# One tile for the keys and queries of a head pair, wider score matmuls, more buffers and a new order in a block-sparse attention and gated convolution kernel

## The chip, the cores and the metric

The kernel runs on one core of a Trainium2 chip. A core has a matrix engine (TensorE, PE in the profile; its weight loads are the row PEld), a vector engine (VectorE, DVE), a scalar engine (ScalarE, ACT), a general engine (GpSimd, POOL) and a queue engine (SyncE, SP). Data move between the main memory and the on-chip memory by DMA; matmuls write to PSUM. The metric is the device time of one execution in microseconds (us). Three runs of the kernel before took 209.91, 210.04 and 211.36 us, so its median is 210.04 us.

## The reference

Attention over 4 batches of 8 heads, 768 tokens and 64 features is followed by a gated convolution network. Only blocks of 32 x 32 tokens that a mask allows count: the block's own neighbours, the first and last row and column of blocks, and three drawn columns per block row.

```python
scores = scale * np.matmul(q, k.transpose(0, 1, 3, 2))      # 4 x 8 x 768 x 768
mask = np.abs(blk_i - blk_j) <= window
mask = mask | (blk_i == 0) | (blk_j == 0) | (blk_i == n_blocks - 1) | (blk_j == n_blocks - 1)
...                                                          # and three drawn blocks per row
scores = np.where(mask, scores, -1000000000.0)
attn = np.exp(scores - np.max(scores, axis=-1, keepdims=True))
attn = attn / (np.sum(attn, axis=-1, keepdims=True) + 1e-09)
x = np.matmul(attn, v)                                       # heads side by side: 4 x 768 x 512
h = np.maximum(x @ w_in, 0.0)                                # 4 x 768 x 1024
conv_out[t] = sum(conv_w[k] * h[t + k - 1] for k in range(3))
out = (h * 1.0 / (1.0 + np.exp(-conv_out))) @ w_out          # 4 x 768 x 512
```

## The kernel before, in words

The kernel computes all scores densely and folds the mask into the score matmul. The 64 features of a head fill 64 rows of the contraction, and 24 more rows (64 to 87) hold the mask: one row per block row, with -8000 in the queries' part and 0 or 1 in the keys' part. That is why the score matmuls have 88 rows.

**Tiles.** Two heads make a pair; there are 16 pairs, four per batch. For a pair the six chunks of 128 keys and the six chunks of 128 queries are held in two tiles: E_t has the even chunks and O_t the odd ones, each of shape [88, 2, 2, 3, 128] (queries or keys, head, chunk, token). Five such slots are used in turn. The first five pairs get there through transposes on PE (`kq_transposes`: k_tr and q_tr, copied out of PSUM by k_cp and q_cp); pairs 5 to 15 get there through DMA transposes on the SP queue (`kq_crossbar`: xb into a staging tile stg, then two copies stg_cp into E_t and O_t). The mask rows of slots 1 and 2 are copied by DVE (m_slot) and those of slots 3 and 4 by DMAs from SP (m_dma); the last batch gets other query rows through small DMAs (m_last).

**Attention.** A unit is eight blocks of 128 x 128 scores, which fill two PSUM banks (tile st). Each half of a unit is one bank of four blocks (operation s, line 744). ACT takes the exponential of the whole unit (exp, line 755), and PE multiplies the eight blocks with the values (av, line 777). There are 144 units. There are only two st tiles, so the scores of a unit wait for the exponential of the unit two before. Blocks are listed per key chunk: for each key chunk the three query chunks of the half sequence that is at work. Neighbouring blocks of a list are merged into one matmul when they share the key chunk and lie side by side in the same tile:

```python
if pieces and pieces[-1][:4] == (P, hh, kc, par) and pieces[-1][4] + pieces[-1][6] == idx:
    pieces[-1] = pieces[-1][:6] + (pieces[-1][6] + 1,)
```

Here par says even or odd tile and idx the place in it. Of the three query chunks two lie in one tile and one in the other, so a matmul is at most 256 columns wide. A list ends where the PSUM bank ends.

**Behind the attention.** For each pair and half sequence DVE takes the reciprocals and normalizes (rcp, norm, lines 694 and 696), the result is transposed into xT by a DMA transpose on SP (x_xb, line 705) or, in a few places, by PE (x_tr, line 715), and then the first matmul of the network runs (f1, line 893), its relu on ACT or DVE (lines 913 and 915), the three-tap convolution and the gate (mul, add, tanh, g1, g2: mostly DVE, tanh on ACT), the second matmul (f2, lines 808 and 823), the copy out of PSUM (ev, lines 326 and 328) and the store.

**The order.** `put_down` writes the program from a string, ORDER. Each entry names an operation by two characters, then its engine by a letter where there is a choice, then the buffer number for each buffer that it takes. Every engine executes its own operations strictly in that order, and so do the DMA queues of SP, ACT and POOL. Semaphore waits between engines follow from which operations touch which tiles. A planner's costs (the functions t_mm, t_act and so on) and due times stand in the code, but the string alone sets the order.

## Time and profile before

| what | value |
|---|---|
| median of three runs | 210.04 us |
| span of the profiled execution, first to last instruction | 207.2 us |
| median of the runs less that span | 2.8 us |
| PE busy | 196.7 us (95%) |
| ACT busy | 189.4 us (91%) |
| DVE busy | 181.5 us (88%) |
| score matmuls (line 744) | 900 |
| granted clock of TensorE | 1.000 |

The profiled execution's own time is told as its span of 207.2 us; what lies around it, before the first and after the last instruction, is put at the 2.8 us by which the median of the runs exceeds it. A busy share counts the time in which at least one instruction of the engine is at work. Matmuls overlap each other, so the time that a matmul costs is read from the distance between the starts of two neighbours and not from its own duration. In the lines below an arrow names what an idle engine waited for.

### The profile page before, as it was taken

How to read it: one execution, taken by the hardware profiler on the slowest of the kernel's cores; microseconds unless marked ns; L12 is line 12 of the kernel's file. 1: busy time of each engine (PE TensorE's matmuls, PEld its weight loads, DVE VectorE, ACT ScalarE, POOL GpSimd, SP SyncE). 2: the span in 40 equal slices, each digit the busy share in tenths (PEclk: the TensorE clock that was granted, in tenths of full speed). 3: DMA queues.
4: the chain of work that ended last, by engine and by line, in shares of the span. 5: the costliest groups of instructions: out<-in, count | busy, mean ns of one | idle time of the engine just before them, and what ended most of it. 6: DMA issues, size and time to landing. Idle time of an engine off the chain costs nothing.

```text
span 207.2 us, 6783 instructions
## 1 busy us (share of the span) xinstructions
PE 196.7 (95%) x2667; PEld 153.7 (74%) x2687; DVE 181.5 (88%) x571; ACT 189.4 (91%) x248; POOL 60.7 (29%) x113
## 2 busy tenths in 40 slices
PE   7799979989999999999999999999999999999993
PEld 7689858867878877777688767777688877795752
DVE  6877759999699998999999998999799959999950
ACT  6899969999999999999999998999899999998841
POOL 8844355446326124500605292700000000000000
PEclk9999999999999999999999999999999999999999
DMA  6999999999998699993597689992511032100415
GB/s 149 170 207 200 173 169 126 141 135 157 158 151 134 98 138 194 181 190 58 77 167 133 88 103 218 170 213 73 175 43 22 19 121 66 29 11 6 156 50 202
DMA packets 54903, 26.26 MB, mean 127 GB/s; under 512 B 40864, under 2 KB 51832, under 8 KB 54872
## 3 DMA queue, kind: packets, MB, share of 16 engines
q0 software_dynamic: 19984, 11.24, 43.5%
q1 hardware_dynamic: 34312, 13.90, 33.8%
q10 hardware_dynamic: 576, 0.69, 1.0%
q8 instruction: 21, 0.34, 0.7%
q14 instruction: 10, 0.08, 0.2%
HBM read 23.08 MB, written 6.29 MB: 142 GB/s over the span
## 4 chain that ended last, share of the span: by engine, by line
PE 56%; ACT 16%; DVE 16%; DMA 5%; issue 4%; SPq 0%; ACTq 0%
PE st L744 16%; PE mix L893 14%; PE mix L823 14%; ACT pt L755 12%; PE av L777 9%; DVE m L947 5%; DMA xT<-xtok 3%; DVE m L957 3%; DMA o2s<-in_q_dram 2%; DVE hE L915 2%; DVE xtok L696 2%; DVE gT L1004 1%; ACT hE L913 1%; DVE m L999 1%; DVE e L328 1%
## 5 line engine op out<-in xcount | busy, mean ns | idle before, releaser
L755 ACT ACTIVATE pt<-st 128x1024 bf16<-128x1024 f32 x144 | 140.2, 1036 | 5.4 <-PE st L744 5.0
L777 PEld LDWEIGHTS <-pt 128*128 128x128 bf16 x1152 | 53.1, 97 | 11.6 <-issue 0.2
L777 PE MATMUL av<-vt,pt 128*128 128x65 bf16 x1152 | 60.6, 193 | 0.3
L893 PE MATMUL mix<-xT,winb 128*128 128x384 bf16 (+2 forms) x288 | 53.8, 308 | 1.1 <-DMA xT<-xtok 0.9
L947 DVE TENSOR_SCALAR m<-hE,cw 128x382 bf16<-128x382 bf16 (+2 forms) x192 | 49.6, 317 | 0.2
L744 PE MATMUL st<-o 88*128 88x128 bf16 (+1 forms) x240 | 44.3, 229 | 1.1 <-ACT pt L755 0.8
L744 PE MATMUL st<-o,e 88*128 88x128 bf16 (+1 forms) x228 | 43.8, 233 | 0.5 <-ACT pt L755 0.4
L744 PE MATMUL st<-e,o 88*128 88x128 bf16 (+1 forms) x224 | 43.0, 234 | 1.2 <-ACT pt L755 1.2
L823 PE MATMUL mix<-woutb,gT 128*128 128x512 bf16 x156 | 43.1, 379 | 0.8
L744 PE MATMUL st<-e 88*128 88x128 bf16 (+1 forms) x208 | 41.5, 239 | 0.6 <-ACT pt L755 0.5
L744 PEld LDWEIGHTS <-o 88*128 88x128 bf16 x464 | 34.4, 97 | 9.4 <-issue 3.0
L744 PEld LDWEIGHTS <-e 88*128 88x128 bf16 x436 | 33.0, 97 | 7.5 <-issue 1.4
L957 DVE TENSOR_TENSOR m<-m 128x764 bf16<-128x764 bf16 (+2 forms) x64 | 33.8, 532 | 0.4
L893 PEld LDWEIGHTS <-winb 128*128 128x128 bf16 x288 | 23.9, 97 | 8.2 <-issue 1.6
L996 ACT ACTIVATE m<-m 128x764 bf16<-128x764 bf16 (+2 forms) x32 | 26.3, 826 | 0.5 <-DVE m L957 0.4
L415 POOL COPY pace<-pt 1x1 bf16<-1x1 bf16 x24 | 8.3, 347 | 47.3 <-ACT pt L755 47.0
L823 PEld LDWEIGHTS <-gT 128*128 128x128 bf16 x184 | 15.4, 97 | 9.0 <-DVE gT L1004 0.5
L915 DVE TENSOR_SCALAR hE<-mix 128x384 bf16<-128x384 f32 x29 | 15.9, 554 | 4.3 <-PE mix L893 4.1
L696 DVE TENSOR_TENSOR xtok<-av,rcp 128x384 bf16<-128x384 f32 (+2 forms) x36 | 18.2, 506 | 0.3
L1004 DVE TENSOR_TENSOR gT<-m,hE 128x764 bf16<-128x764 bf16 (+3 forms) x36 | 18.1, 508 | 0.3
L913 ACT ACTIVATE hE<-mix 128x384 bf16<-128x384 f32 (+2 forms) x35 | 16.9, 503 | 1.6 <-PE mix L893 1.2
L238 POOL DMA_DIRECT2D nat<-in_q_dram x23 | 16.9, 736 | 3.0 <-issue 2.8
(80 smaller groups left out, 156.4 us busy)
## 6 DMA issues: line engine op xcount, KB each, us to landing
out_dram<-o2s SPq DMA_DIRECT2D x22, 256.0 KB
vn<-in_v_dram POOLq DMA_DIRECT2D x16, 192.0 KB, 5.3
nat<-in_k_dram POOLq DMA_DIRECT2D x15, 192.0 KB, 5.1
nat<-in_q_dram POOLq DMA_DIRECT2D x7, 192.0 KB, 4.8
winb<-in_moe_w_in_dram POOLq DMA_DIRECT2D x2, 512.0 KB, 8.1
woutb<-in_moe_w_out_dram POOLq DMA_DIRECT2D x4, 256.0 KB, 5.8
nat<-in_q_dram POOLq DMA_DIRECT2D x8, 96.0 KB, 5.3
xT<-xtok SPq DMA_TRANSPOSE x32
```

The lines of the kernel that those rows point to most:

```text
L696: nm = op("norm", {"DVE": t_dps(128 * C)}, lambda e: nc.vector.tensor_tensor(out=xtok_t[xk.index][:, 0:C].rearrange("p c h d -> p h c d"), ...
L744: nc.tensor.matmul(out=st[:, 128 * x:128 * (x + n_)], lhsT=QK[kc % 2][s][0:88, 1, hh, kc // 2, :], rhs=QK[par][s][0:88, 0, hh, idx:idx + n ...
L755: nc.scalar.activation(out=pt_t[ptb.index], in_=st_t[stb.index], func=AF.Exp, bias=0.0, scale=0.125)
L777: nc.tensor.matmul(out=o[:, off:off + 65], lhsT=pt_t[ptb.index][:, 128 * x:128 * x + 128], rhs=V_t[vslot_b[P].index][:, hh, kc, 0:65], sta ...
L823: nc.tensor.matmul(out=acc(), lhsT=gT_t[gb.index][:, ffc, 128 * t:128 * t + 128], rhs=woutb[:, ffc, :], start=(ffc == 0), stop=(ffc == NFF ...
L893: nc.tensor.matmul(out=mix_t[hb.index][:, w1 * y:w1 * y + w1], lhsT=winb[:, fc, 128 * ffc:128 * ffc + 128], rhs=xT_t[xt_buf[n].index][:, f ...
L913: i = nc.scalar.activation(out=dst, in_=src, func=AF.Relu, bias=0.0, scale=0.5)
L915: i = nc.vector.tensor_scalar(out=dst, in0=src, scalar1=0.5, scalar2=0.0, op0=ALU.mult, op1=ALU.max)
L947: i = nc.vector.tensor_scalar(out=m_t[cb.index][:, x, y, 0:w], in0=hE_t[heb.index][:, f0 + y, t0 + x:t0 + x + w], scalar1=cw[:, x, f0 + y: ...
L957: nc.vector.tensor_tensor(out=m[:, a_, :, 0:w], in0=m[:, a_, :, 0:w], in1=m[:, b_, :, 0:w], op=ALU.add)
L996: th = [op("tanh", {"ACT": t_act(2 * w) + 0.04}, lambda e, cb=cb, w=w: nc.scalar.activation(out=m_t[cb.index][:, 0, :, 0:w], in_=m_t[cb.in ...
L1004: i = nc.vector.tensor_tensor(out=gT_t[gtb.index][:, f0:f0 + 2, t0:t1], in0=m_t[cb.index][:, 0, :, 0:w], in1=hE_t[heb.index][:, f0:f0 + 2, ...
```

## The change

Four things are changed together.

1. E_t and O_t become two strided views of one tile QK_t of shape [88, 2, 2, 6, 128], in which even and odd chunks alternate. The three query chunks of a half sequence then lie side by side. The query chunks are listed in the order 0, 1, 2 or 3, 4, 5, so that up to three neighbours are merged: the pieces of a bank of four blocks become 384 + 128, 256 + 256 or 128 + 384 columns wide, where they were 256 + 128 + 128 in some order.
2. The mask rows of slots 3 and 4 are copied by one DMA each where there were two, and the last batch's query rows by one DMA per pair where there were two.
3. Seven constants grow: stg 2 to 3, nat 4 to 6, vn 3 to 4, pt 6 to 8, xtok and rcp (one constant) 3 to 4, xT 3 to 4, o2s 4 to 5.
4. ORDER is replaced.

The new ORDER, read entry by entry, holds the same operations apart from the six DMAs fewer. These change their engine, in net numbers: three relus, one ev, one k_cp and three q_cp go from ACT to DVE; one cast_k, one v_cp and one x_cp go from DVE to ACT. ACT's operations up to the first exponential are, before: m_q, m_h1, cast_q, k_cp, cast_k, cast_q, k_cp, k_cp, q_cp, q_cp, m_h1; and after: m_q, m_h1, cast_k, cast_q, m_h1, k_cp, cast_k, q_cp, cast_q, k_cp. DVE's operations around the first two normalizations are, before: rcp, k_cp, he_zero, cw, v_cp, k_cp, k_cp, q_cp, q_cp, norm, v_cp, diag, rcp, diag, diag, norm; and after: rcp, diag, norm, v_cp, k_cp, q_cp, rcp, q_cp, norm. The first f1 stands behind the same number of score and value operations in both. POOL's loads keep their order but for a few neighbours that change places, with as many paces (small copies that hold POOL until a load has landed). At the end of SP's list the stores of two earlier output tiles stand behind those of the last batch's tiles 2 and 3, where before none did.

```diff
-    NSLOT, NSTG, NNAT, NVN, NPT, NXK, NXT, NHE, NCV, NGT, NOS = 5, 2, 4, 3, 6, 3, 3, 2, 4, 2, 4
-
-    E_t = many(NSLOT, [88, 2, 2, 3, 128], BF16, "e")
-    O_t = many(NSLOT, [88, 2, 2, 3, 128], BF16, "o")
+    NSLOT, NSTG, NNAT, NVN, NPT, NXK, NXT, NHE, NCV, NGT, NOS = 5, 3, 6, 4, 8, 4, 4, 2, 4, 2, 5
+
+    QK_t = many(NSLOT, [88, 2, 2, 6, 128], BF16, "qk")
+    E_t, O_t = [[t[:, :, :, x:6:2] for t in QK_t] for x in range(2)]
...
-            else:
-                mr.append(op("m_dma", {"SP": 0.75}, lambda e, t=t, s=s: nc.sync.dma_start(out=t[s][64:88], in_=t[0][64:88]),
-                             T(4.5 * s - 2.5) + 0.1 * x, [m_h1[x], m_kh[x]], dma=("hw", 0.6)))
+        if s >= SLOT_DMA:
+            mr = 2 * [op("m_dma", {"SP": 0.75}, lambda e, s=s: nc.sync.dma_start(out=QK_t[s][64:88], in_=QK_t[0][64:88]),
+                         T(4.5 * s - 2.5), m_h1 + m_kh + m_k, dma=("hw", 0.6))]
...
-                    dcopy(e, t[slot.index][0:64, 1, hs[0]:hs[-1] + 1].rearrange("p h c s -> p (h c s)"), src)
+                    dcopy(e, t[slot.index][0:64, 1, hs[0]:hs[-1] + 1], src.rearrange("p (h c s) -> p h c s", h=len(hs), c=3))
...
-    blk_order = {0: [(0, 0, 0), (0, 1, 2), (1, 0, 1)], 1: [(1, 1, 0), (1, 2, 2), (0, 2, 1)]}
+    blk_order = {0: [(0, 0, 0), (1, 0, 1), (0, 1, 2)], 1: [(1, 1, 0), (0, 2, 1), (1, 2, 2)]}
...
-                if pieces and pieces[-1][:4] == (P, hh, kc, par) and pieces[-1][4] + pieces[-1][6] == idx:
-                    pieces[-1] = pieces[-1][:6] + (pieces[-1][6] + 1,)
+                at = 2 * idx + par
+                if pieces and pieces[-1][:3] == (P, hh, kc) and pieces[-1][3] + pieces[-1][5] == at:
+                    pieces[-1] = pieces[-1][:5] + (pieces[-1][5] + 1,)
...
-                                     lhsT=QK[kc % 2][s][0:88, 1, hh, kc // 2, :],
-                                     rhs=QK[par][s][0:88, 0, hh, idx:idx + n_, :].rearrange("p c s -> p (c s)"),
+                                     lhsT=QK_t[s][0:88, 1, hh, kc, :],
+                                     rhs=QK_t[s][0:88, 0, hh, at:at + n_, :].rearrange("p c s -> p (c s)"),
```

105 lines of the change are left out of this document (51 added, 54 removed).

## The prediction

> **What bounds the kernel now.** I read the busy shares and the chain first, and then the busy time of each engine by stretches of the span, because a share over the whole span hides where an engine has room.
>
> ```profile
> PE 196.7 (95%) x2667; PEld 153.7 (74%) x2687; DVE 181.5 (88%) x571; ACT 189.4 (91%) x248; POOL 60.7 (29%) x113
> PE 56%; ACT 16%; DVE 16%; DMA 5%; issue 4%; SPq 0%; ACTq 0%
> core 0: us, PE busy (x) PEld busy (x) DVE busy (x) ACT busy (x) POOL busy (x), PEclk, DMA share, GB/s
> 7.00:28.00 21.00, 18.41 (x323) 16.70 (x321) 16.61 (x49) 20.82 (x25) 10.51 (x20) 1.00 1.32 190
> 28.00:45.00 17.00, 15.46 (x217) 12.20 (x216) 14.24 (x46) 15.39 (x22) 8.57 (x19) 1.00 1.22 132
> 45.00:190.00 145.00, 143.55 (x1955) 110.83 (x1971) 135.70 (x408) 139.93 (x175) 35.52 (x62) 1.00 0.72 116
> 190.00:204.00 14.00, 13.42 (x125) 8.61 (x124) 9.85 (x42) 8.65 (x20) 0.00 (x0) 1.00 0.34 125
> 204.00:207.20 3.20, 0.00 (x0) 0.00 (x0) 0.00 (x0) 0.12 (x1) 0.00 (x0) 1.00 0.33 113
> ```
>
> The rows tell of three regimes. From 7 to 28 us ACT is busy 20.82 of 21.00 us and PE idles 2.59: the exponentials set the pace, since there is no network work yet. From 28 to 45 us PE idles 1.54 us and ACT 1.61. From 45 to 190 us PE idles 1.45 us of 145, while ACT has 5.07 us free and DVE 9.30. So in the long middle only less work on PE, or less waiting of PE, can shorten the run. Before 45 us PE idles 4.13 us together, and this is all that a better start can give as long as the first score keeps its place; work that ACT and DVE shed in the middle gives nothing by itself.
>
> What PE and ACT waited for before 45 us is in the table of waits (total, times, longest):
>
> ```profile
> PE st L744 <- ACT pt L755: 2.6, 7, 1.2
> ACT pt L755 <- PE st L744: 1.6, 1, 1.6
> PE mix L893 <- DMA xT<-xtok: 0.9, 1, 0.9
> ```
>
> PE's largest waits are for exponentials that free a score tile (2.6 us; the longest, 1.2 us, is for the very first one), and one wait of 0.9 us for the transposed input of the first f1. The scores queued behind that f1 on PE were late, and ACT stood for 1.6 us.
>
> **The wider matmuls.** The chain shows runs of PE in one piece, and the groups show the score loads.
>
> ```profile
> 126.98 0.89 PE st L744 x12
> 127.87 1.30 PE mix L893 x8
> 145.90 1.73 PE mix L823 x8
> L744 PEld LDWEIGHTS <-o 88*128 88x128 bf16 x464 | 34.4, 97 | 9.4 <-issue 3.0
> L744 PEld LDWEIGHTS <-e 88*128 88x128 bf16 x436 | 33.0, 97 | 7.5 <-issue 1.4
> 126.82 0.22 PE L744 MATMUL st<-e 88*128 88x128 bf16 x1
> 126.88 0.27 PE L744 MATMUL st<-o 88*128 88x256 bf16 x1
> 126.99 0.22 PE L744 MATMUL st<-e,o 88*128 88x128 bf16 x1
> ```
>
> Twelve score matmuls are four banks of four blocks of 128 columns, 2048 columns, in 0.89 us. Eight matmuls of 512 columns are 4096 in 1.73 us, and eight of 384 are 3072 in 1.30 us, so a column costs 1.73/4096 = 0.00042 us at most, and 2048 of them 0.86 us. Twelve matmuls thus carry about 0.03 us beside their columns, 2.5 ns each; the two decimals allow 1 to 4 ns, and I take 3. There are 464 + 436 = 900 score matmuls. In the seven full segments (1008 of the 1152 blocks, 252 banks) three per bank become two, which is 252 fewer; in the segment with two query chunks 24 banks go from four to two, 48 fewer; the last one keeps its 48. So 900 become 600, with the same columns: 300 x 3 ns = **0.9 us** less on PE (0.3 to 1.2). Neighbours start 0.06 and 0.11 us apart, closer than the 97 ns of one load: the loads are hidden already, and 300 loads fewer free nothing more.
>
> [...]
>
> **The start.** ACT's list up to the first exponential in the timeline:
>
> ```profile
> 3.61 0.51 ACT L326 COPY o<-o 24x384 bf16<-24x384 bf16 x1
> ...
> 5.11 0.51 ACT L326 CAST nat<-o2s 128x384 bf16<-128x384 f32 x1
> 6.12 0.35 ACT L326 CAST nat<-o2s 128x192 bf16<-128x192 f32 x1 [0.50 <-DMA o2s<-in_q_dram]
> 6.50 0.47 ACT L326 COPY o<-mix 64x384 bf16<-64x384 bf16 x1
> 7.00 0.74 ACT L326 COPY e<-av 64x384 bf16<-64x384 bf16 x2
> 7.75 0.26 ACT L326 COPY o<-av 64x128 bf16<-64x128 bf16 x1
> 8.03 0.51 ACT L326 COPY e<-e 24x384 bf16<-24x384 bf16 x1
> 8.57 20.79 ACT L755 ACTIVATE pt<-st 128x1024 bf16<-128x1024 f32 x22
> ```
>
> In the new order ACT does, from 3.61 on, m_h1 0.51, cast_k 0.51, cast_q 0.35, m_h1 0.51, k_cp 0.47, cast_k 0.51, q_cp 0.26, cast_q 0.35, k_cp 0.47: together 3.94 us, so the first exponential can start at 7.55 instead of 8.57, 1.0 us earlier. The query load that held ACT at 6.12 is by then in. The unit's scores (0.89/2 = 0.45 us) can begin when the q_cp is done, at about 6.7, and so they are there. But the copies that ACT sheds are now DVE's, and the scores of the third to sixth unit stand behind them; the one tile adds waits too, since a score that reads even chunks may be made to wait for the copy of the odd ones between them. Bounds: 0 to 1.0 us; I take **0.6 us**, past the middle, because the copies moved are short (0.26 to 0.47). Behind the late scores only av and the next scores would queue on PE. While ACT sets the pace every bit of this counts to the end: PE's work behind it is fixed.
>
> **The first f1.** Its late operand was the normalization of the second pair:
>
> ```profile
> 15.73 0.18 DVE L694 RECIPROCAL rcp<-av 128x6 f32<-128x6 f32 x1
> 19.88 0.56 DVE L696 TENSOR_TENSOR xtok<-av,rcp 128x384 bf16<-128x384 f32 x1
> 20.62 0.57 DVE L388 TENSOR_SCALAR diag<-ident,cw 128x128 bf16<-128x128 bf16 x3
> 21.21 1.25 DVE L388 TENSOR_SCALAR diag<-ident,cw 128x128 bf16<-128x128 bf16 x6
> 22.15 0.55 DVE L696 TENSOR_TENSOR xtok<-av,rcp 128x384 bf16<-128x384 f32 x1
> 22.73 6.50 DMA xT<-xtok
> ```
>
> The first normalization came four microseconds after its reciprocal, because copies stood between them on DVE, and the second behind nine diag instructions (0.57 + 1.25 us). Its DMA transpose left at 22.73 and landed 6.50 us later, among loads that kept the DMA engines full. The new order puts one diag ahead of the first norm, one q_cp between the second rcp and its norm, and the other diags behind, so both transposes leave SP's queue over a microsecond earlier, more than the 0.9 us that PE waited. With the f1 at its old place in PE's list I count **0.9 us**; bounds 0 (transposes as late under earlier loads) and 1.6 (ACT's wait). What is late next is the norm of the third pair, which cannot precede its last av.
>
> **The engine changes.** Where an operation can go to either, these rows tell the price.
>
> ```profile
> L913 ACT ACTIVATE hE<-mix 128x384 bf16<-128x384 f32 x27 | 12.9, 505 | 0.8 <-PE mix L893 0.6
> L915 DVE TENSOR_SCALAR hE<-mix 128x384 bf16<-128x384 f32 x29 | 15.9, 554 | 4.3 <-PE mix L893 4.1
> L328 DVE COPY o<-stg 64x1536 bf16<-64x1536 bf16 x11 | 6.5, 595 | 0.3
> L328 DVE COPY vt<-vn 128x768 bf16<-128x768 bf16 x16 | 5.6, 359 | 0.1
> L328 DVE COPY e<-mix 64x768 bf16<-64x768 bf16 x4 | 2.2, 550 | 1.7 <-PE mix L468 1.6
> ```
>
> ACT sheds three relus (1.5 us) and five more operations and takes three, about 2 us in net; DVE gains three relus (1.7 us), an ev, a k_cp and three q_cp and sheds three, about 2.7 us. After 45 us ACT's relief is worth nothing, as PE is last there; before, two relus fewer ahead of the 36th exponential may return part of the 0.64 us that PE still idles: **0.3 us** (0 to 0.6). DVE's 2.7 us lie in its 9.30 us of idle time between 45 and 190 us and cost 0; without that cover, 2.7.
>
> **The strided tile.** The copies into QK_t write runs of 128 elements with gaps. The value copy writes runs of 64 into rows of 66 and takes 359 ns for 768 elements, half of them again for 1536 in 595: gaps do not slow it. I take 0. The other end is the rate of the copies out of PSUM, 550 ns for 768.
>
> **Other moves.** More buffers only lift waits of loads and copies that PE does not stand behind: 0. The six DMAs fewer are cheap and lie in SP's queue between the stores and transposes: 0. Two stores more at the end of SP's queue are 0.5 MB:
>
> ```profile
> 202.00:204.00 2.00, 1.71 (x16) 1.28 (x14) 0.42 (x1) 0.84 (x2) 0.00 (x0) 1.00 0.93 344
> ```
>
> At 344 GB/s they take 1.5 us; they are issued before PE's last 2 us, so I take 0 (0 to 1.5). A new order brings waits of its own on PE; the old one has 1.45 us in its middle, and I add **0.3 us** (0 to 2).
>
> **Sum.** -0.9 - 0.6 - 0.9 - 0.3 + 0.3 = -2.4 us against the profiled span of 207.2, so 204.8; with the 2.8 us around it, 207.6, against the median of 210.04 (-1.2%).
>
> **Rivals.** (1) The start is given back: the first units wait for DVE's copies, or f1 for its transposes, and only the wider matmuls count: 210.04 - 0.9 = 209.1. For it speaks that DVE, too, is in the start's chain. (2) Slower: larger pools let loads start earlier, and they collide with the DMA transposes on which every segment's first f1 depends. Each of the eight segments then waits 0.9 us as the first does now: +6.3, less 0.9 and 0.6, gives 214.8; over 1% slower from five segments on. For it speak the 6.50 us landing and the DMA share of 1.22 to 1.32 before 45 us, against it the pacing copies, which are as many as before, and the share of 0.72 later. (3) Slower: DVE becomes the bound. If the 22 staged copies ran at the PSUM rate, each would take 1.10 instead of about 0.58 us, +11.4; with the 2.7 moved that is 14.1, 4.8 over DVE's idle 9.30, so 210.04 + 4.8 - 2.4 = 212.4. It decides from about 0.30 us more per copy. (4) The loads were not hidden and each of the 300 frees up to its 97 ns: 29 us, 181. [...] That neighbours start 0.06 us apart speaks against it.
>
> **How the numbers follow.** Forecast 0.53, rivals 0.25, 0.12, 0.09 and 0.01. About 1% is what a measurement of this kernel can tell from no change: 207.9 to 212.1. Of the forecast 0.50 lies below, 0.03 within; with rival 4 and a little of rival 1 faster gets 0.52, within 0.27, slower 0.21. The forecast's own bounds, with all savings whole, reach 4.4 us, to 205.6. The range 204.8 to 212.0 takes in the forecast, rival 1 and about half of the slower cases.
>
> **What would show it.** 600 score matmuls, 384-column ones starting 0.16 us before their neighbour; the first exponential near 8.0 us; no wait of f1 for xT before 45 us; PE idle under 3 us before 45 us and under 2 us from 45 to 190; staged copies near 0.58 us. The prediction falls if PE waits for DVE or DMA in the middle.

## The result, and the profile after

The changed kernel took 219.26 us (median of four runs, 215.53 to 221.36) beside 210.7 us for the kernel before on the same chip: a ratio of **1.0318**, 95% interval 1.0244 to 1.0392. On another chip, later, it took 215.98 us, ratio 1.0238 (1.0180 to 1.0296). It is slower by 2 to 3%; forecast was 1.2% faster. Here and below a time is the median of all runs, while a ratio and its interval compare the fast runs alone (here 217.48 and 215.53 us of the changed kernel) and leave out the slow ones, those over 1.5% above the fastest of the same kernel, which is why 219.26 beside 210.7 us is not 1.0318. The profiled execution took 217.48 us with a span of 215.7, against 207.2 before.

The busy shares, then PE's busy share and its granted clock in 40 equal slices of the span, in tenths (the page of the changed kernel):

```profile
PE 200.3 (93%) x2369; PEld 143.3 (66%) x2387; DVE 183.8 (85%) x578; ACT 188.6 (87%) x243; POOL 57.3 (27%) x113
PE   7999949999996999999999999999699999999993
PEclk9999988999998899999999999999999999999999
```

The span grew by 8.5 us, PE's busy time by 3.6 (196.7 before) and so its idle time by 4.9. Two dips of the clock stand in the third line, where this profile of the kernel before has none, each right behind or at a dip of PE. By stretches:

```profile
core 0: us, PE busy (x) PEld busy (x) DVE busy (x) ACT busy (x) POOL busy (x), PEclk, DMA share, GB/s
7.00:28.00 21.00, 19.47 (x285) 15.07 (x284) 17.33 (x59) 20.53 (x24) 9.28 (x18) 1.00 1.33 182
28.00:45.00 17.00, 14.54 (x161) 10.10 (x161) 12.02 (x37) 12.53 (x16) 10.83 (x21) 0.90 0.97 122
45.00:190.00 145.00, 139.00 (x1675) 98.25 (x1688) 130.92 (x384) 133.68 (x164) 31.15 (x62) 0.99 0.80 116
```

Up to 28 us PE idles 1.53 us, 1.06 less than before. From 28 to 45 it is 2.46 (1.54 before), with the clock at 0.90 in the mean, and from 45 to 190 it is 6.00 (1.45 before). The gain of the start is lost at 28 us, and the larger loss sits in the middle, where the kernel before hardly stopped.

What came as forecast: the matmuls and the copies (groups of the changed kernel), and the first exponential (ACT's timeline).

```profile
L742 PE MATMUL st<-qk 88*128 88x256 bf16 (+2 forms) x600 | 92.9, 270 | 1.8 <-ACT pt L753 1.1
L328 DVE COPY qk<-stg 64x1536 bf16<-64x1536 bf16 x22 | 11.9, 550 | 4.2 <-DMA stg<-nat 3.9
```
```profile
7.44 3.77 ACT L753 ACTIVATE pt<-st 128x1024 bf16<-128x1024 f32 x4
```

There are 600 score matmuls; the staged copies take 550 ns in the strided tile, not more than before (595 for those of O_t); the first exponential starts 1.13 us earlier. The second row has the new thing in its last column: VectorE stood 3.9 us for staged transposes. What PE waited for (the table of waits):

```profile
PE mix L891 <- DMA xT<-xtok: 3.2, 3, 2.0
PE mix L891 <- DVE hE L913: 2.1, 1, 2.1
PE mix L891 <- ACT o2s L326: 1.4, 2, 1.3
PE mix L821 <- DVE gT L1002: 0.8, 1, 0.8
```

These are three stops. **The first**, and behind it the second, in PE's timeline:

```profile
27.34 0.33 PE L891 MATMUL mix<-xT,winb 128*128 128x384 bf16 x1
28.38 0.32 PE L891 MATMUL mix<-xT,winb 128*128 128x384 bf16 x1 [0.72 <-DMA xT<-xtok]
30.70 2.08 PE L891 MATMUL mix<-xT,winb 128*128 128x384 bf16 x6 [2.00 <-DMA xT<-xtok]
...
61.90 1.14 PE L891 MATMUL mix<-xT,winb 128*128 128x384 bf16 x6
...
66.60 1.14 PE L891 MATMUL mix<-xT,winb 128*128 128x384 bf16 x6 [2.12 <-DVE hE L913]
```

The first f1 starts at 27.34 us (28.07 before) and waits 0.72 and 2.00 us for the pieces of xT (0.9 in all before). Six matmuls then take 2.08 us, at a granted clock of 0.50, where six at full clock take 1.14: the stop is paid a second time. **The second stop**, at 64 us, is PE waiting for a relu that frees its PSUM bank, and VectorE's timeline tells why the relu is late:

```profile
58.95 0.56 DVE L913 TENSOR_SCALAR hE<-mix 128x384 bf16<-128x384 f32 x1 [0.98 <-PE mix L891]
62.27 1.12 DVE L328 COPY qk<-stg 64x1536 bf16<-64x1536 bf16 x2 [2.76 <-DMA stg<-nat]
```

Two staged copies of pair 7 are next in line and wait 2.76 us for their DMA transpose; the relu stands behind them. **The third stop**, near 150 us, is two waits:

```profile
152.47 1.04 PE L821 MATMUL mix<-woutb,gT 128*128 128x512 bf16 x4 [0.79 <-DVE gT L1002]
156.29 0.81 PE L891 MATMUL mix<-xT,winb 128*128 128x384 bf16 x4 [1.26 <-ACT o2s L326]
```

### The profile page after: what moved, and what is told of

It is laid out like the page before. It is cut to its first block, busy times and chain, and to the rows that moved or that the text cites. A ratio compares the mean times of both kernels' runs of the same rounds, so it can differ in the third digit from the quotient of the medians.

```text
span 215.7 us, 6173 instructions
## 1 busy us (share of the span) xinstructions
PE 200.3 (93%) x2369; PEld 143.3 (66%) x2387; DVE 183.8 (85%) x578; ACT 188.6 (87%) x243; POOL 57.3 (27%) x113
## 4 chain that ended last, share of the span: by engine, by line
PE 62%; DVE 15%; DMA 13%; ACT 4%; issue 3%; POOL 1%; ACTq 0%; SPq 0%; POOLq 0%; DVEq 0%
PE st L742 19%; PE mix L891 15%; PE mix L821 12%; PE av L775 12%; DVE qk L328 6%; DMA stg<-nat 4%; DMA xT<-xtok 4%; DMA nat<-in_q_dram 3%; DVE m L945 3%; DVE m L955 2%; ACT pt L753 2%; DVE xtok L693 1%; DMA out_dram<-o2s 1%; DVE vt L328 1%; PE mix L806 1%
## 5 line engine op out<-in xcount | busy, mean ns | idle before, releaser
L742 PE MATMUL st<-qk 88*128 88x256 bf16 (+2 forms) x600 | 92.9, 270 | 1.8 <-ACT pt L753 1.1
L742 PEld LDWEIGHTS <-qk 88*128 88x128 bf16 x600 | 49.0, 98 | 22.5 <-issue 3.9
L891 PE MATMUL mix<-xT,winb 128*128 128x384 bf16 (+2 forms) x288 | 56.4, 314 | 6.8 <-DMA xT<-xtok 3.2
L775 PE MATMUL av<-vt,pt 128*128 128x65 bf16 x1152 | 59.5, 194 | 0.3
L913 DVE TENSOR_SCALAR hE<-mix 128x384 bf16<-128x384 f32 x32 | 17.6, 553 | 9.5 <-PE mix L891 7.5
L414 POOL COPY pace<-pt 1x1 bf16<-1x1 bf16 x24 | 5.7, 237 | 57.8 <-ACT pt L753 57.5
L328 DVE COPY qk<-stg 64x1536 bf16<-64x1536 bf16 x22 | 11.9, 550 | 4.2 <-DMA stg<-nat 3.9
L326 ACT COPY o2s<-mix 128x512 f32<-128x512 f32 (+1 forms) x15 | 8.4, 561 | 5.7 <-DMA out_dram<-o2s 3.4
L997 DVE TENSOR_SCALAR m<-m 128x764 bf16<-128x764 bf16 (+3 forms) x36 | 11.7, 327 | 1.4 <-ACT m L994 0.8
L328 DVE COPY qk<-mix 64x256 bf16<-64x256 bf16 (+3 forms) x28 | 11.4, 407 | 1.1 <-PE mix L505 0.6
```

Of the source, the lines that this page charges most:

```text
L328: nc.vector.tensor_copy(out=dst, in_=src)
L742: nc.tensor.matmul(out=st[:, 128 * x:128 * (x + n_)], lhsT=QK_t[s][0:88, 1, hh, kc, :], rhs=QK_t[s][0:88, 0, hh, at:at + n_, :].rearrange( ...
L775: nc.tensor.matmul(out=o[:, off:off + 65], lhsT=pt_t[ptb.index][:, 128 * x:128 * x + 128], rhs=V_t[vslot_b[P].index][:, hh, kc, 0:65], sta ...
L891: nc.tensor.matmul(out=mix_t[hb.index][:, w1 * y:w1 * y + w1], lhsT=winb[:, fc, 128 * ffc:128 * ffc + 128], rhs=xT_t[xt_buf[n].index][:, f ...
L913: i = nc.vector.tensor_scalar(out=dst, in0=src, scalar1=0.5, scalar2=0.0, op0=ALU.mult, op1=ALU.max)
```

## The experiments

Two theories were set against each other. **A**: the change is sound, and its order makes DMA arrivals late or asks for them too early, at three places that can be named. **B**: something spread out is at fault, the wide tile, or an order that is short of DMA or engine time all through, so that every repair only moves the wait. Ratios are to the kernel before, executed beside each version on the same chip. ORDER is a string of codes, so edits of it are shown as lists of operations.

### The wide tile alone, and the changed kernel again

```diff
 kernel before, old ORDER, old pools
+one tile QK_t, block order 0,1,2 / 3,4,5, pieces up to 384 columns
+m_last in two DMAs as before, of 2 and 1 chunks
```

> The kernel before with one part of the change alone: keys and queries of a head pair lie in one tile, and the pieces of the score matmuls are merged over it (600 score matmuls, up to 384 columns, in place of 900); the order, the pool sizes and the number of DMAs are those of before. Theory A (the wide matmuls and the strided copies do no harm, the loss is in the new order): score matmuls 384 wide start 0.16 us apart, the staged copies stay near 0.55 us, and the time falls by 0.3 to 1.2 us against the kernel before, 0.9 by the 3 ns that each of 300 saved matmuls costs; ratio 0.994 to 0.999. Rival B (reading and writing the one tile costs something, in longer matmuls, copies or waits for both parities): 0 to 3 us slower, ratio 1.000 to 1.014.

Measured: 211.34 us, ratio **0.9965** (0.9917 to 1.0012). The ratio stands for 0.7 us less, near the 0.9 of the forecast, but its interval takes in no change, and the two medians (211.34 beside 210.24 us) point the other way. So a gain is not shown; what is shown is that no loss of the size of the result is in the tile.

> The changed kernel itself once more, beside the three kernels that follow, because the first comparisons were made on other chips. Both theories: 216 to 221 us, and two stretches of 3.41 us at half clock in most executions, each right behind a stretch in which TensorE stood for more than 2 us.

Measured: 215.98 us, just below what both theories said; its profile (span 214.8) has two stretches at half clock again. It is the second yardstick for what follows. Its second stop shows in another place, though (a row of its waits; the kernel above has 3.2 us there and 2.1 for the relu, hE):

```profile
PE mix L891 <- DMA xT<-xtok: 4.4, 3, 2.1
```

The longest of these waits, 2.1 us, ends at 59.87 us at a later f1, and none there is for the relu. So in one and the same kernel the lateness at 55 to 65 us comes out at different instructions.

### The first stop: what is issued ahead of the transposes

SEQ lists the loads that POOL issues; each waits until the load three places ahead has landed.

```diff
-    SEQ = "nq0 nq1 k4 q4 w0 v4 w1 nq2 w2 k5 q5 w3 v5 nq3 k6 q6 v6 k7 q7 v7 nq4"
+    SEQ = "nq0 nq1 k4 q4 nq2 v4 w0 w1 w2 k5 q5 w3 v5 nq3 k6 q6 v6 k7 q7 v7 nq4"
-            d, buf, src = seq[x - 3]
+            d, buf, src = seq[x - {4: 1, 5: 2, 6: 2}.get(x, 3)]
```

> The changed kernel with only the sequence of loads on POOL's queue altered: the third small query load and the values of pair 4 go first, and the first two pieces of the second weight matrix (512 KB) wait for the loads before them, so that they are issued behind the three transposes of the first xT instead of ahead of the second and third. Theory A (a transpose lands only when the loads issued ahead of it have gone through the same DMA engines, at about 200 GB/s): the third transpose lands near 27.5 to 28.5 us in place of 30.66, the first f1 waits at most 1 us for xT in place of 3.2, the stretch of half clock at 30.5 us is gone, and the time falls by 3 to 4.5 us (2.2 to 2.7 of wait and 1.7 for 3.41 us at half clock) to about 215.5. Rival B (the transposes are slow by themselves, or the wait only moves): it lands after 30 us, and the time changes by less than 1 us.

Measured: 216.06 us, ratio 1.0272 (1.0212 to 1.0333). The third transpose, issued in both at 22.4 us, landed so (DMA issues of the changed kernel, then of this one, with the time to landing at the end of the line):

```profile
xT<-xtok SPq DMA_TRANSPOSE x1, 8.3
```
```profile
xT<-xtok SPq DMA_TRANSPOSE x1, 4.8
```

So it landed at 27.2 instead of 30.7 us, the first f1 did not wait, and the half clock at 30 us was gone. The first stop comes from the loads issued ahead of the transposes. But the time hardly moved, for a reason that PE's timeline of this run shows:

```profile
44.20 0.61 PE L505 MATMUL mix<-ident,nq 128*128 128x128 bf16 x4 [5.24 <-DMA nq<-in_q_dram]
```

A small query load, later in the sequence, had become the last one.

In the changed kernel the third transpose thus landed at 30.66 us, just behind the last load issued ahead of it (30.36), and in the run with loads held back 3.5 us earlier. That the loads issued ahead of a transpose set its landing is in keeping with both times; by what mechanism, no run here tells.

The query load was then moved up:

```diff
-    ... nq2 v4 w0 w1 w2 k5 q5 w3 v5 nq3 k6 ...
+    ... nq2 v4 w0 w1 nq3 w2 k5 q5 w3 v5 k6 ...
```

> As the first experiment on the loads (the second weight matrix issued behind the transposes of the first xT), with the fourth small query load moved up ahead of the third piece of that matrix, so that it isn't late in its turn. Theory A (loads ahead of a transpose delay it, and the first experiment only lost its gain to the late query load, 5.2 us): the first f1 waits under 1 us, the transpose of queries near 39 us waits under 0.5 us, no half clock before 60 us, and the time falls by 3 to 4.5 us against the changed kernel, to about 215. Rival B (some other load is late in turn, the DMA engines have no room before 45 us): less than 1.5 us gained.

Measured: 218.79 us, ratio 1.0378 (1.0328 to 1.0429). The first stop stayed away, but PE then waited 2.5 us for staged copies at 45 us and 4.1 us for VectorE at 57 us: rival B's reading. Holding loads back leaves the DMA engines less busy at 28 to 36 us (a share of 0.60, 1.07 in the changed kernel), and what comes later is later. To see whether it is the amount, 512 KB were taken away altogether; the result then lacks the part of the second product that these weights make:

```diff
-            ld_wout.append(dma("ld_wout", "POOL", lambda x=x: woutb[:, 2 * x:2 * x + 2], ...
+        if x < 2:
+            ld_wout.append(op("ld_wout", {"POOL": 1.0}, lambda e, x=x: nc.gpsimd.memset(woutb[:, 2 * x:2 * x + 2], 0.0), ...
```

> The changed kernel with 512 KB of DMA work taken away: the first two of the four pieces of the second weight matrix are set to zero by POOL instead of being loaded (this part of the FFN's second product is therefore left out of the result; all instructions of the other engines stay). Nothing else is altered. Theory A (in the first 65 us the DMA engines have no room, and the new order asks for its transposes and staged tiles sooner than the loads ahead of them let them through): the third transpose of the first xT lands at 28 us or before (30.66 in the changed kernel), the first f1 waits under 0.5 us, and, since the loads behind it move up by up to 2.6 us (512 KB at 200 GB/s), the later wait near 57 to 64 us shrinks below 1 us too; no half clock before 100 us; time down by 5 to 8 us to 208.5 to 212. Rival B (it is SP's and VectorE's order, whatever the DMA load): only the first wait shrinks, the later one stays at 2 us or more, time down by 2 to 4 us.

Measured: 213.86 us, ratio 1.0136 (1.0065 to 1.0207), by the ratios 2 to 4 us below the changed kernel. The transpose landed at 27.9, and f1 did not wait. The second stop stayed, 3.0 us, and VectorE's timeline says what it was now:

```profile
52.94 0.55 DVE L328 COPY qk<-stg 64x1536 bf16<-64x1536 bf16 x1 [1.27 <-DMA stg<-nat]
55.26 0.36 DVE L328 COPY vt<-vn 128x768 bf16<-128x768 bf16 x1 [1.76 <-DMA vn<-in_v_dram]
```

With half a megabyte less to load, transposes and values still came late at 50 to 55 us. So the second stop is not a lack of DMA time in the first 30 us.

### The second stop: first tries

VectorE's staged copies of pair 7 behind the relus; then the same with two transposes of xT ahead of staged ones on SP; then the first f1 and all that hangs on it two exponentials later:

```diff
-DVE: relu(fg 1), stg_cp 7, stg_cp 7, mul ..., relu(fg 3)
+DVE: relu(fg 1), mul ..., relu(fg 3), stg_cp 7, stg_cp 7
-SP: xb 6k, xb 6q, x_xb(hp 1), x_xb(hp 2), xb 7k, x_xb(hp 3), xb 7q
+SP: xb 6k, x_xb(hp 1), xb 6q, x_xb(hp 2), x_xb(hp 3), xb 7k, xb 7q
```

> The changed kernel with only two staged copies (keys and queries of one pair, about 62 us) put behind the relus of the f1 results on VectorE. Theory A (the copies stood in line ahead of the relu and waited 2.76 us for their transpose, and TensorE's bank came free late): the wait of f1 for hE near 64 us (2.3 us) and the half clock at 68 us (3.41 us, worth 1.7) are gone, and the time falls by 3 to 4 us to about 215.5. Rival B (VectorE is short of time in this stretch whatever its order): the wait moves to the scores or to gT, the time falls by less than 1.5 us.

> The changed kernel with two repairs at 45 to 65 us only: the two staged copies behind the relus on VectorE, and two transposes of xT put ahead of staged transposes on SP's queue (loads and the first f1 untouched). Theory A (the second stop comes from the order in which SP and VectorE serve staged tiles and xT): waits of f1 between 50 and 70 us under 0.5 us in sum (2.1 to 2.9 in the changed kernel), half clock there gone, time down by 2.5 to 4.5 us to 212 to 216. Rival B (the DMA engines are behind in this stretch): the wait moves to the next score or f1 there, less than 1.5 us gained.

> The changed kernel with the same loads in the same sequence, but the first segment's FFN instructions (f1, relus, convolution, second product) put about two exps later on every engine, the delay running out over the next 19 exps, and with av matmuls that were ready moved ahead of them. Theory A (the new order places the first f1 before the DMA engines can bring xT): the first f1 waits under 0.8 us, no half clock at 30 us, no new wait before 50 us, time down by 2 to 4 us against the changed kernel (216 to 219): 212.5 to 216. Rival B (the delayed FFN work is missed later, by the second segment): the gain reappears as waits at 50 to 75 us, less than 1.5 us gained.

Measured: 217.94, 217.78 and 214.99 us. The runs of the first two spread from 215.10 to 220.32 and from 214.37 to 218.15 us, and there is no ratio for them; the last has 1.0199 (1.0142 to 1.0256). In the first the relu's wait was gone, and f1 waited 2.0 us for xT at 55 us instead; in the second f1 waited 1.9 us at 58 us for an eviction behind a copy of pair 6. In the third the wait of f1 at 64 us fell to 0.2 us, but PE ran short of work at 26 to 46 us (4.33 us idle, 2.80 in the changed kernel). Each time the wait moved: rival B's sign, but no cause yet. The move in the first one can't be put down to its edit, since the second profile of the unedited kernel has the same wait for xT.

Next all copies that wait for DMA were put behind the evictions, without and with the rest, and the mirror was tried in the kernel before: pair 7's copies put early there, as in the new order.

```diff
-DVE: v_cp 6, stg_cp 6, v_cp 7, stg_cp 6, ev, ev, relu, stg_cp 7, stg_cp 7, ..., relu
+DVE: ev, ev, stg_cp 6, relu, stg_cp 6, v_cp 6, ..., stg_cp 7, stg_cp 7, relu, ..., v_cp 7
```

> The changed kernel with only VectorE's order altered: nine staged copies (of four pairs, near 55, 60, 105 and 151 us) are put behind the relus and evictions that TensorE's banks wait for, each still ahead of the first score that needs it. Queues, loads and the other engines are as in the changed kernel. Theory A (the stops after the first come from staged copies that stand too early in VectorE's line, waiting for their transposes): no wait of f1 for hE or o2s on VectorE above 0.5 us, the waits at 57 to 64, 108 and 151 us gone (4 to 5 us in sum with the half clock behind the first), only the first f1's wait for xT and a wait for xT near 57 us left; time down by 3 to 5 us against the changed kernel (216 to 219), to 212 to 215. Rival B (the copies are then late for the scores): less than 1.5 us gained, and the scores wait for qk near 60 us.

> The kernel before with one thing taken over from the new order: the two staged copies of pair 7 stand on VectorE right behind the first relus of the second segment instead of behind the relu of f1's fourth group (three to five exps earlier, near 58.5 us in place of 61.4). Theory A (copies that stand early in VectorE's line hold up the relus that free TensorE's banks): a wait of f1 for hE of 0.7 to 2.5 us near 61 us, time 0.7 to 3 us above the kernel before. Rival B (the order of the copies doesn't matter, VectorE's idle time takes it up): within 0.5 us of the kernel before.

> The changed kernel with its loads untouched and every DMA arrival near 45 to 65, 105 and 150 us asked for later: on VectorE the staged copies as in the run with VectorE's order alone, and the value copies of pairs 6 and 7 as well, which stood ahead of two evictions and waited for the last load of this stretch; on SP two transposes of xT ahead of staged ones, and one store earlier. Theory A (in the first 65 us both kernels run at the pace of the DMA engines; the new order puts copies that wait for late arrivals ahead of evictions in VectorE's line, and the value copy of pair 7 is the one that was left in the run before): TensorE's waits between 50 and 70 us fall from 3 to 4 us to under 1.2 us in sum and those of 145 to 165 us to under 1 us, the first f1's stop (2 to 3 us) stays; time 211.5 to 214.5 us (changed kernel 216 to 219). Rival B (the loss in this stretch has nothing to do with the order of VectorE and SP): 215.5 us or more, with waits above 2 us at 50 to 70 us.

The first of these left v_cp 6 and 7 where they were; in it, in the third and in all runs with the repair of the third stop two small mask DMAs (m_last) of SP also change places. Measured: 217.48 us (ratio 1.0348, 1.0266 to 1.0430); 212.56 (1.0022, 0.9966 to 1.0079); 215.82 (1.0298, 1.0213 to 1.0382). The theory of the early copies fell: moving them back does not win the time, and moving them forward in the kernel before costs nothing that can be measured; there the copies, at 58.94 us, did not wait for their transposes. So a copy's place in line seems to matter here only where its data are late, and the question became why the transposes are late.

### The third stop

```diff
+SP: an earlier output's store directly behind another one, near 130 us
-DVE: stg_cp 15, ..., g2 (gT)
+DVE: ..., g2 (gT), stg_cp 15
 ACT: ev into the o2s buffer that this store has freed
```

> The changed kernel with, between 130 and 156 us, one store issued earlier, so that the result at 155.65 us finds another o2s buffer that is free, and one staged copy of VectorE put behind the product for gT. Theory A (the two stops of TensorE at 151.5 and 154.7 us come from a store that stood behind five transposes on SP's queue, and from a copy that waited 1.14 us for its transpose): the two waits (0.95 and 1.42 us) are gone and the time falls by 1 to 2.4 us to about 217.5. Rival B (the loads of the last batch are late as such): TensorE stops at the next result or score instead, less than 0.5 us gained.

Measured: 216.17 us, ratio 1.0262 (1.0204 to 1.0319). Both waits are gone from the profile (one for xT of 0.3 us is in their place). Against the two measurements of the changed kernel, 1.0318 and 1.0238, its worth in time is open.

### All together, and where it was decided

> The changed kernel with all repairs: the loads' sequence, the two staged copies behind the relus, two transposes of xT on SP's queue ahead of staged transposes near 45 to 55 us, the store and the staged copy near 150 us. Theory A (the change lost 8 to 9 us to three stops of TensorE and the half clock behind two of them, and the rest of it is sound): no wait of TensorE over 1 us between 15 and 190 us, granted clock 0.99 or more, span 204 to 207.5 us, time 206 to 209.5 us, below the kernel before by 0 to 2%. Rival B (the new order is tight all through, each repair only moves the wait): 212 us or more.

> The changed kernel with the later first f1, the two repairs at 45 to 65 us and the repair near 150 us (store and staged copy), loads in their own sequence. Theory A (three stops, each of its own): no wait of TensorE over 1 us between 15 and 190 us, granted clock 0.99 or more, time 206.5 to 210.5 us. Rival B (the loads are late as a stream, and each repair moves the wait): 212 us or more, with a wait of over 1 us of TensorE between 40 and 75 us that the changed kernel hasn't got.

> The changed kernel with VectorE's order as in the run before, and further: the two first pieces of the second weight matrix leave POOL's queue behind the transposes of the first xT, but without a hole in the stream of loads (the values of pair 4 and the third small query load ahead of them); two transposes of xT ahead of staged ones on SP's queue near 45 to 55 us; one store earlier near 130 us. Theory A (the change is sound and lost its time to DMA arrivals that its order put too late or asked for too early): first f1 waits under 1 us, third transpose of the first xT lands by 28.5 us, no wait of TensorE above 1 us between 15 and 190 us, time 206.5 to 210.5 us. Rival B (the stretch from 40 to 65 us is short of DMA time in this order whatever the queues' order): 211.5 us or more with a wait above 1 us there.

Measured: 217.40 us (1.0283, 1.0237 to 1.0329), 216.48 (1.0266, 1.0219 to 1.0313) and 215.66 (1.0219, 1.0148 to 1.0289): rival B three times. In each a wait near 45 to 70 us was left. The first used the second sequence of loads, the second the later f1, the third a sequence that proved too weak: its third transpose landed near 30 us.

What all had in common shows on SP's queue. SP's timeline and waits of the changed kernel:

```profile
17.23 26.12 SPq L702 DMA_TRANSPOSE xT<-xtok  x4
43.44 7.65 SPq L582 DMA_TRANSPOSE stg<-nat  x4
```
```profile
SPq L702 <- DVE hE L913: 19.4, 1, 19.4
```

VectorE's timeline has the normalization that this transpose reads (the row of waits names one of VectorE's relus near it):

```profile
41.59 0.55 DVE L693 TENSOR_TENSOR xtok<-av,rcp 128x384 bf16<-128x384 f32 x1
```

and SP's timeline of the kernel before:

```profile
33.73 1.22 SPq L583 DMA_TRANSPOSE stg<-nat  x1
39.70 1.59 SPq L705 DMA_TRANSPOSE xT<-xtok  x1
41.39 1.23 SPq L583 DMA_TRANSPOSE stg<-nat  x1
```

In the new order the fourth transpose of xT (the first of the second segment) heads SP's queue and stands there for 19.4 us, until VectorE has normalized its input at 42 us. Behind it wait the two staged transposes of pair 5. Their loads, in POOL's timeline and among the DMA issues of the changed kernel:

```profile
30.94 0.71 POOL L238 DMA_DIRECT2D nat<-in_k_dram  x1 [0.27 <-DMA nq<-in_q_dram]
31.77 0.76 POOL L238 DMA_DIRECT2D nat<-in_q_dram  x1
```
```profile
nat<-in_k_dram POOLq DMA_DIRECT2D x1, 192.0 KB, 4.5
nat<-in_q_dram POOLq DMA_DIRECT2D x1, 192.0 KB, 4.7
```

They landed at 35.4 and 36.5 us, and their transposes left at 43.44 and after. The kernel before has this transpose of xT between the two: it issued the first staged one at 33.73, as soon as it could, and the second at 41.39. From 34 to 44 us the DMA engines of the changed kernel were less busy than before, and from 44 to 60 more (stretches of the changed kernel, then of the kernel before; the last two columns are the DMA share and GB/s):

```profile
34.00:44.00 10.00, 9.96 (x131) 7.57 (x130) 9.29 (x30) 9.74 (x13) 6.42 (x13) 1.00 0.93 114
44.00:60.00 16.00, 15.01 (x176) 10.27 (x177) 14.29 (x38) 15.18 (x18) 5.16 (x12) 1.00 1.35 159
```
```profile
34.00:44.00 10.00, 9.32 (x147) 7.49 (x145) 9.32 (x28) 9.94 (x16) 5.32 (x12) 1.00 1.33 141
44.00:60.00 16.00, 15.52 (x227) 12.57 (x226) 14.14 (x42) 16.00 (x19) 7.01 (x12) 1.00 1.25 157
```

That alone did not stop PE in the changed kernel: the copies of pair 5, at 53.20 us, waited for nothing. What came late there was the second transpose of pair 7, which left at 57.23 us although its load had landed at 53.1; transposes of xT stood before it.

Two runs tell the place on the queue apart from a lack of DMA time. The first has the loads resequenced (the second weight matrix behind the keys and queries of pair 5, then four loads in flight), the later copies, and on SP the exchanges near 45 to 55 us and the earlier store; the second is the same kernel with one instruction moved.

```diff
-    SEQ = "nq0 nq1 k4 q4 w0 v4 w1 nq2 w2 k5 q5 w3 v5 nq3 k6 q6 v6 k7 q7 v7 nq4"
+    SEQ = "nq0 nq1 k4 q4 nq2 v4 k5 q5 w0 nq3 w1 v5 w2 k6 w3 q6 v6 k7 q7 v7 nq4"
-            d, buf, src = seq[x - 3]
+            d, buf, src = seq[x - {3: 3, 4: 1, 5: 2, 6: 2, 7: 3, 8: 3}.get(x, 4)]
```

> The run beside this one with the loads resequenced too: the pieces of the second weight matrix, which nothing needs before about 46 us, go behind the keys and queries of pair 5, nothing but one small query load and the values of pair 4 is issued between the transposes of the first xT and their landing, and from then on four loads are in flight in place of three. Theory A: third transpose of the first xT lands by 28 us, first f1 waits under 0.8 us, no half clock between 15 and 190 us, waits of TensorE between 20 and 70 us under 3 us in sum (7.5 to 8.6 in the changed kernel, 3.7 in the kernel before), time 207 to 210.5 us. Rival B (the loads held back at 24 us are late later, whatever the sequence): 212 us or more, with a wait of over 1 us between 35 and 70 us.

```diff
-SP: x_xb(next segment, hp 0), xb 5k, xb 5q, xb 6k
+SP: xb 5k, xb 5q, x_xb(next segment, hp 0), xb 6k
```

> The run with resequenced loads and later copies, with one instruction moved: on SP's queue the first transpose of the second segment's xT, which waits for a result of VectorE until about 38 to 42 us, goes behind the two staged transposes of pair 5, whose loads landed at 32.4 and 33.8 us there (35.5 and 36.5 in the changed kernel), as it stands in the kernel before. Theory A (in the changed kernel this one instruction at the head of SP's queue leaves the DMA engines without work near 36 to 44 us and crowds all later transposes and loads into 44 to 60 us, which is what stops TensorE there): pair 5's transposes are issued by 35.5 us, loads between 40 and 50 us land in 5 to 8 us in place of 9 to 12, the wait of a score for qk at 50 us (3.24 us) and the half clock behind it are gone, waits of TensorE at 35 to 70 us under 2.5 us in sum (6.8 in that run), time 208.5 to 212.5 us. Rival B (the stretch is short of DMA time as such): 214.5 us or more, with a wait of over 1.5 us at 45 to 70 us.

Measured: 217.21 us (ratio 1.0350, 1.0307 to 1.0393), then **212.72 us** (1.0116, 1.0067 to 1.0165). PE's timeline of the first, and SP's timeline of the second:

```profile
53.84 0.38 PE L742 MATMUL st<-qk 88*128 88x384 bf16 x2 [3.08 <-DVE qk L328]
```
```profile
32.09 3.31 SPq L582 DMA_TRANSPOSE stg<-nat  x2
39.10 1.18 SPq L702 DMA_TRANSPOSE xT<-xtok  x1
```

In the first run pair 5's transposes left at 39.47 us, the second landed 11.59 us after its issue, and a score waited 3.08 us for the copies. With the transposes at 32.09 us that wait is gone, as is the half clock behind it. The loads issued between 40 and 47.2 us land in 5.4 to 7.6 us instead of 9 to 12. The stretches of the first run and then of the second, laid as above:

```profile
34.00:44.00 10.00, 9.58 (x138) 7.42 (x137) 9.88 (x31) 9.88 (x13) 7.04 (x14) 1.00 1.29 152
44.00:60.00 16.00, 11.47 (x101) 6.93 (x103) 9.36 (x23) 11.32 (x13) 4.50 (x10) 0.89 1.54 135
```
```profile
34.00:44.00 10.00, 9.81 (x154) 7.75 (x152) 9.88 (x33) 9.89 (x12) 6.76 (x14) 1.00 1.38 191
44.00:60.00 16.00, 15.21 (x178) 10.16 (x177) 14.34 (x37) 15.27 (x19) 4.79 (x11) 1.00 1.36 156
```

The ratio falls by 2.3 points for the place of one instruction, with intervals that lie apart, though the two runs were on different chips. That is theory A in the kernel of these two runs. Idle DMA engines are the lesser part of it: the share from 34 to 44 us rises only from 1.29 to 1.38. What is not shown: this move alone in the changed kernel, without the new sequence of loads and the later copies, was not run, so that it makes the second stop there is argued. And 1.2% is left to the kernel before; PE idles 5.07 us from 45 to 190 us in that run (1.45 before), in waits near 103, 109 and 150 us that were not pursued.

### The repair of the first stop in the kernel before

```diff
 kernel before with the one tile and the wide matmuls
 pacing of the loads as in the first repair of the first stop
+    SEQ = "nq0 nq1 k4 q4 nq2 v4 w0 w1 nq3 w2 k5 q5 w3 v5 k6 q6 v6 k7 q7 v7 nq4"
```

> The kernel before with the one tile and the wide score matmuls, in the old order with the old pools, and the second weight matrix issued behind the transposes of the first xT, as in the repair above. Theory A (the same delay costs the kernel before its first wait of f1 for xT, 1.0 us in its profile, and now and then a stretch of half clock): that wait is under 0.3 us, and the time is 0.5 to 3 us below the kernel before (0.9 for the matmuls, 1.0 for the wait, 0 to 1.7 for half clock); ratio 0.985 to 0.998. Rival B (the old order hides that wait, or another load is late in turn): ratio 0.996 to 1.01.

Measured: 211.59 us, ratio 1.0011 (0.9965 to 1.0056): rival B. The wait of f1 for xT is not in its profile any more, and nothing is gained that can be measured. No version here beats the kernel before for certain.

## Why the prediction was wrong, step by step

**The wider matmuls** (-0.9): right in count and in spacing (384-column matmuls start 0.16 us before their neighbour); -0.7 by the ratio of the run with the tile alone, whose interval holds both the 0.9 and zero, so the time saved is not shown.

**The start** (-0.6): right. The first exponential gained 1.13 us, and 0.6 us of it was left at the twenty-first (26.75 against 27.36 us in the timelines), just ahead of the first f1.

**The first f1** (-0.9, bounds 0 and -1.6): wrong, and this step failed first. That the transposes "leave SP's queue over a microsecond earlier" was right (17.23, 19.91 and 22.39 against 20.46, 22.73 and 24.23 us). I took their time to landing for fixed. It depends on the loads issued ahead, and the third landed at 30.66, where before f1 had its pieces by 29.4. The wait grew from 0.9 to 2.7 us at this f1: about 0.7 us of that because f1 itself starts earlier, the rest because xT lands later. A loss was not even among the bounds. The run with those loads held back shows that they make the wait. Why the same list of loads delays the transposes more than before stays open.

**Other moves** (0): wrong. I costed the six DMAs fewer and the two late stores of SP's queue, and not which instruction of the new order stands ahead of which on that queue. A transpose of xT waits there for 19.4 us ahead of two staged ones whose loads have landed. The last pair of runs prices its place at 2.3% (4.5 us between their medians), in a kernel with other loads; its price in the changed kernel itself was not measured.

**The new order's own waits** (+0.3, 0 to 2): mis-sized. From 45 to 190 us PE idles 6.00 us in place of 1.45, +4.6, in waits for relus, evictions and gT that VectorE and ACT delivered late.

**The clock**: no step had it. Two stretches of 3.41 us at half clock hold 3.19 and 3.41 us of PE's busy time; at full clock that would be half, about 3.3 us, as an estimate from the granted clock of 0.50. With 4.9 us more of idle time that is 8.2 of the 8.5 us. The 0.3 us left are busy time at full clock, where the wider matmuls should have taken 0.9 away; why is open. The account holds for these two profiles: in other executions the old order runs below full clock too, at a mean of 0.91 from 15 to 35 us in the profile with the tile alone and 0.86 in that with pair 7's copies early.

**The engine changes and the strided tile** (-0.3 and 0): VectorE's busy time rose by 2.3 us (2.7 forecast) and did not bound; 550 ns per staged copy means that rival 3 has no ground. ACT's relief could show nothing, since ACT waited for PE: from 28 to 45 us it stood 4.47 us (1.61 before).

**The rivals**: the second, 214.8 us, had the time nearly right and half of the mechanism, loads ahead of DMA transposes. It put it in every segment and on the larger pools; the trace has it at the first f1 and, in part by way of SP's queue, at 45 to 65 us. The larger pools are not ruled out: in the kernel before POOL waited 1.75 us for a free vn buffer and issued that load at 11.27 us, in the changed kernel it left at 8.73 without a wait. No run has the pools alone. My sentence that the prediction falls if PE waits for DVE or DMA in the middle named the sign, and the chance of 0.12 was too small for a change whose order touched every queue.

## What to carry to other kernels

In a new order read each DMA queue as a list of its own: for every entry when its data are ready, and what stands behind it. An entry that waits at the head of the queue delays what is behind it: here one stood for 19.4 us, and two transposes behind it, whose loads had landed by 36.5 us, left at 43.44 and after. In the last pair of runs the loads issued as all of it came at once landed late as well (9 to 12 us against 5.4 to 7.6). A transpose that is issued earlier need not land earlier: the third one here left 1.8 us earlier (22.39 against 24.23) and landed over 1 us later (30.66 against 29.4), behind the same loads. A repair that holds loads back must be followed through to the last load. Run an order's suspected waits one by one before fixing them together: here most fixes only showed the next wait, and with all of the work kept the time came near the old one only when one instruction of SP's queue was moved as well.

## What the runs showed of the hardware that was not expected

**The clock fell to half for 3.41 us behind stops of PE that were shorter than that, on what looks like a grid of 3.41 us.** Both stretches at half clock between 13 us and the last matmuls of the changed kernel are 3.41 us long, and they begin at 30.48 and 68.03 us, 11 times 3.41 apart. Stretches of that kernel, laid on that grid (the third column from the end is the clock):

```profile
27.07:30.48 3.41, 0.92 (x6) 0.44 (x5) 0.17 (x1) 2.45 (x3) 1.78 (x4) 1.00 1.10 160
30.48:33.89 3.41, 3.19 (x12) 1.68 (x12) 1.63 (x5) 0.16 (x1) 2.17 (x6) 0.50 0.88 104
64.62:68.03 3.41, 1.25 (x8) 0.69 (x8) 3.34 (x12) 1.92 (x3) 0.00 (x0) 1.00 0.00 0
68.03:71.44 3.41, 3.41 (x34) 2.46 (x33) 2.73 (x12) 3.13 (x4) 1.77 (x4) 0.50 0.14 15
```

and of the run with only pair 7's copies moved:

```profile
151.36:154.77 3.41, 1.68 (x16) 0.89 (x15) 1.41 (x4) 1.50 (x3) 0.00 (x0) 1.00 0.41 143
154.77:158.18 3.41, 3.41 (x41) 2.46 (x37) 2.97 (x10) 3.41 (x7) 0.00 (x0) 1.00 0.17 54
```

A stretch in which PE was idle for 2.49 or 2.16 us was followed by one at half clock; the one with 1.73 us idle was not. Of all other stretches of the changed kernel on this grid, from 13 to 204 us, the one at 153.36 us has the most idle time, 1.25 us, and none of them was followed by half clock. The half clock can also go on, as it did in the first run with loads held back:

```profile
38.10:41.51 3.41, 0.85 (x18) 0.57 (x14) 1.23 (x3) 1.69 (x3) 2.67 (x4) 1.00 1.11 145
41.51:44.92 3.41, 0.72 (x6) 0.66 (x7) 0.08 (x1) 0.00 (x0) 1.31 (x4) 0.50 1.52 190
44.92:48.33 3.41, 3.41 (x35) 2.71 (x34) 3.05 (x10) 2.05 (x2) 2.32 (x5) 0.50 1.30 155
48.33:51.74 3.41, 3.21 (x54) 2.50 (x52) 2.77 (x9) 3.40 (x4) 0.87 (x2) 1.00 1.26 160
```

PE was idle for 2.56 and 2.69 us in the first two of these, and the second and third are at half clock. So, as an estimate from these rows, a stop of 2.16 us costs up to 1.7 us more (half of 3.41) when it lies within one stretch of the grid, and nothing beyond itself when a border of the grid leaves 1.73 us or less of it on either side.

**With one transpose waiting at the head of a queue, the loads of another queue came late.** In the two runs that differ in its place alone, the loads that POOL issued between 40 and 47.2 us took 9 to 12 us to land when it stood first and 5.4 to 7.6 when it stood third, and the DMA share from 44 to 60 us was 1.54 and 1.36.
